# Two attention chunks scored in one burst of TensorE, and three relu copies after it on ScalarE

## The chip, the cores and the metric

The kernel runs on one core of a Trainium2 chip. A core has five engines that run side by side, each with its own queue that it works off in order: TensorE (PE in the profile; its weight loads have a row of their own, PEld), VectorE (DVE), ScalarE (ACT), GpSimd (POOL) and SyncE (SP), which here only issues DMAs. An engine waits for another through semaphores. The metric is the device time of one execution in microseconds; the median over several executions is what two kernels are compared by.

## The reference, cut to what matters

Four batches of 768 tokens pass through two layers. The first is a recurrent attention with a decay for each of 8 heads of 64 numbers; it is computed here in chunks of 128 tokens. The second adds a low-rank mix along the tokens (rank 32) and an MLP from 512 to 2048 and back:

```python
for t in range(S):                                  # S = 768, for each batch and head
    state = gamma * state + outer(k[t], v[t])
    y[t] = scale * q[t] @ state                     # 8 heads of 64 -> x of 512 columns
u = x + (x.T @ U @ V).T                             # U: 768 x 32, V: 32 x 768
out = u + relu(u @ w_ch1) @ w_ch2                   # w_ch1: 512 x 2048, w_ch2: 2048 x 512
```

In chunks, the attention of a chunk is a masked product of its queries and keys (the scores) with its values, plus its queries times the state that the chunks before left behind. The decay is folded into scaled copies of q and v.

## The kernel before, in words

**The order is written out by hand.** The program runs inside a manual schedule, so each engine works in the order in which the Python code emits its instructions. Batch 0's attention runs first, alone, from a list of steps. After it, the MLP of batch b carries the attention of batch b + 1 with it: `mlp_pieces(b)` gives a list of pieces, each with a cost, and `weave` (L404) walks through that list and emits, between two pieces, every function whose mark has been reached. A mark is a share of the MLP's total cost; one whole MLP is 1.0, and the pieces' costs add up to 41.5.

**The pieces of one MLP.** First come 16 up pieces for 512 tokens, each of four matmuls of 512 columns (L356), then 16 up pieces for the other 256 tokens, each of four matmuls of 256 columns, then 24 down pieces of four matmuls of 512 columns (L379). An up piece ends in a relu copy out of its accumulator in PSUM into `gT`: every third one is on VectorE (L361), the others are on ScalarE (L363). Four down pieces make one output chunk, which VectorE adds to `u` (L386) and a DMA that GpSimd issues stores (L342). The accumulators (`mlp`) rotate over three banks of PSUM, so the matmuls of a piece wait for the copy out of the piece that had its bank before, three pieces earlier while nothing else takes a bank.

**One chunk of attention.** `prep_chunk` scales and casts k, q and v on GpSimd (L81, L83) and lets SyncE issue further loads. `turn_chunk` transposes k and q: in batch 1 with TensorE (L230) and a copy by ScalarE (`kT`) and one by VectorE (`qT`), in batches 2 and 3 with a DMA that SyncE issues (L226); `kT` and `qT` have three buffers each. `score` (L234) makes eight matmuls that use 64 of the 128 rows (L239) into one of two accumulators, `R[ci % 2]`, each two banks of PSUM; VectorE then multiplies them by the causal mask into `a` (L242). `mix` (L247) writes into the same `R[ci % 2]`: queries times the state before (L257, 64 rows; none in chunk 0), `a` times the values (L262, 128 rows), and ScalarE copies the result into `x` (L265). Then four matmuls add the chunk's keys times values to the state in PSUM (L274), and two ScalarE copies bring the state out as `ns` (L280), which the next chunk's `mix` reads.

After the six chunks, `lr_proj` (L293), `lr_expand` (L302) and `lr_turn` (in batch 1 on TensorE, L323; later by DMA, L317) make the next batch's `u` and `uT`.

**The marks.** `AT` (L684) holds for each batch the place of the first score, the step from chunk to chunk, the distance from a chunk's score to its mix, and how far ahead `prep_chunk` and `turn_chunk` stand. So in the kernel before, each chunk's scores stand alone between pieces of the MLP, and its mix follows 0.045 or 0.05 of an MLP later.

Of the kernel before, what the change touches and what calls it, by code (L numbers as in the profile page):

```python
# [16 lines left out]
def kernel(  # L17
# [42 lines left out]
    def bank(tag, dtype=fp32):  # L60
        n_bank[0] += 1
        return psum.tile([P, 2048 // (4 if dtype == fp32 else 2)], dtype,
                         tag=tag, name=f"{tag}_{n_bank[0]}", bufs=BANKS[tag])
# [143 lines left out]
    def load_w2(j):  # L207
        nc.gpsimd.dma_start(
            out=w2b[:, ds(4 * j, 4)],
            in_=moe_w_ch2[ds(512 * j, 512)].rearrange("(m p) n -> p m n", p=P))  # L210

    xs = {}
    live = {}
    bts = {}
# [19 lines left out]
    def score(b, ci):  # L234
        r, kT, qT = R[ci % 2], bts.pop(("k", b, ci)), bts["q", b, ci]
        for hp in range(4):
            for i in range(2):
                ri = ds(D * i, D)
                nc.tensor.matmul(r[:, i, ts(hp, P)], kT[ri, hp], qT[ri, hp],  # L239
                                 start=True, stop=True)  # L240
        a = rmid.tile([P, 2, 4, P], bf16, tag="a4", name=f"a4_{b}_{ci}", bufs=3)
        nc.vector.tensor_tensor(  # L242
            a, r.rearrange("p i (n m) -> p i n m", n=4),
            mask[:, None, None, :].to_broadcast([P, 2, 4, P]), op=ALU.mult)
        live["a", b, ci] = a

    def mix(b, ci):  # L247
        if ci == 0:
            open_x(b)
        r, qT = R[ci % 2], bts.pop(("q", b, ci))  # L250
        kb, vb, a = pre.pop(("k", b, ci)), pre.pop(("v", b, ci)), live.pop(("a", b, ci))
        if ci:
            st = live.pop(("state", b, ci - 1))
            for hp in range(4):
                for i in range(2):
                    ri = ds(D * i, D)
                    nc.tensor.matmul(r[:, i, ts(hp, D)], qT[ri, hp],  # L257
                                     st[ri, ts(hp, D)], start=(hp == 0), stop=False,
                                     skip_group_check=True)
        for hp in range(4):  # L260
            for i in range(2):
                nc.tensor.matmul(r[:, i, ts(hp, D)], a[:, i, hp], vb[:, 2 * hp + i],  # L262
                                 start=(ci == 0 and hp == 0), stop=True,
                                 skip_group_check=True)
        evac("A", xs[b][:, ci].rearrange("p (n i e) -> p i n e", i=2, e=D),  # L265
             r[:, :, :256].rearrange("p i (n e) -> p i n e", e=D))
        if ci == NCK - 1:
            return
        if ci == 0:
            live["st_p", b] = bank("st")  # L270
        st_p = live["st_p", b]
        for hp in range(4):
            h2 = ds(2 * hp, 2)
            nc.tensor.matmul(st_p[:, ts(hp, P)], kb[:, h2], vb[:, h2],  # L274
                             start=(ci == 0 and hp == 0), stop=True,
                             skip_group_check=True)
        ns = rmid.tile([P, 4 * D], bf16, tag="ns", name=f"ns_{b}_{ci}")
        for i in range(2):
            ri = ds(D * i, D)
            evac("A", four(ns)[ri], four(st_p)[ri, :, ri])  # L280
        live["state", b, ci] = ns
# [62 lines left out]
    def mlp_pieces(b):  # L344
        gT = gtp.tile([P, NM, S], bf16, tag="gT", name=f"gT_{b}")
        pieces = []
        n = [0]

        def up(m, lo, sz):
            def f():  # L350
                g_p = begun.pop((b, m, lo), None)
                c0 = 2 if g_p is not None else 0
                if not c0:
                    g_p = bank("mlp")
                for c in range(c0, NCB):
                    nc.tensor.matmul(g_p[:, :sz], w1b[:, c, ts(m, P)],  # L356
                                     uTs[b][:, c, ds(lo, sz)], start=(c == 0),
                                     stop=(c == NCB - 1))
                n[0] += 1
                if n[0] % 3 == 0:  # L360
                    nc.vector.tensor_relu(gT[:, m, ds(lo, sz)], g_p[:, :sz])  # L361
                else:
                    nc.scalar.activation(gT[:, m, ds(lo, sz)], g_p[:, :sz],  # L363
                                         AF.Relu)
            return f

        for m in range(NM):
            pieces.append((0.864, up(m, 0, LO)))
        for m in range(NM):
            pieces.append((0.432, up(m, LO, S - LO)))  # L370
        hold = {}

        def down(j, m0, n0=0, nn=DM):
            def f():
                if m0 == 0:
                    hold[j, n0] = bank("mlp")
                ch = hold[j, n0]
                for m in range(m0, m0 + 4):
                    nc.tensor.matmul(ch[:, :nn], gT[:, m, ts(j, P)],  # L379
                                     w2b[:, m, ds(n0, nn)],  # L380
                                     start=(m == 0), stop=(m == NM - 1))
                if m0 == NM - 4:
                    o_sb = outp.tile([P, DM], fp32, tag="o_sb",
                                     name=f"o_{b}_{j}_{n0}")[:, :nn]
                    n = ds(n0, nn)
                    nc.vector.tensor_tensor(o_sb, ch[:, :nn], us[b][:, j, n],  # L386
                                            op=ALU.add)
                    if n0:
                        nc.sync.dma_start(out=out[b, ts(j, P), n], in_=o_sb)
                    else:  # L390
                        stores.append((nc.gpsimd, out[b, ts(j, P), n], o_sb))
            return f

        for j in range(NCK):
            if (b, j) == (B - 1, NCK - 1):
                for n0, nn in ((0, 384), (384, 128)):
                    for m0 in range(0, NM, 4):
                        pieces.append((0.864 * nn / DM, down(j, m0, n0, nn)))
                continue
            for m0 in range(0, NM, 4):  # L400
                pieces.append((0.864, down(j, m0)))
        return pieces
# [18 lines left out]
    def part(f, *args):  # L421
        return lambda: f(*args)
# [258 lines left out]
    for ci in range(3):  # L681
        prep_chunk(1, ci)

    AT = {1: (0.47, 0.068, 0.045, 0.07, 0.04), 2: (0.20, 0.085, 0.05, 0.20, 0.12),  # L684
          3: (0.13, 0.10, 0.05, 0.20, 0.12)}
    LR = {1: (0.875, 0.905, 0.95, 0.975), 2: (0.71, 0.75, 0.83, 0.89)}
    marks = {b: [] for b in range(B)}

    def mark(at, f, *args):
        marks[int(at)].append((at % 1.0, part(f, *args)))  # L690
# [3 lines left out]
        lr_proj(b)  # L694

    for b in range(1, B):
        s0, step, dm, dp, dt = AT[b]
        for ci in range(NCK):
            s_at = b - 1 + s0 + step * ci
            if (b, ci) >= (1, 3):  # L700
                mark(s_at - dp, prep_chunk, b, ci)
            mark(s_at - dt, turn_chunk, b, ci)
            mark(s_at, score, b, ci)
            mark(s_at + dm, mix, b, ci)
            if b > 2:
                mark(b - 2 + 0.25 + 0.1 * ci, open_chunk)
        l0, l1, l2, l3 = LR[min(b, 2)]
        mark(b - 1 + l0, mixed, b)
        mark(b - 1 + l1, lr_expand, b, 0, 4)
        mark(b - 1 + l2, lr_turn, b, 0)  # L710
        mark(b - 1 + l3, lr_turn, b, 2)
        mark(b + 0.02, lr_expand, b, 4, 2)
        mark(b + 0.06, lr_turn, b, 4)
# [35 lines left out]
```

## Time and profile before

| | us |
|---|---|
| median of 3 runs (234.75 to 238.98) | 234.82 |
| the profiled execution | 233.89 |
| its span, first to last instruction | 232.1 |

| engine | busy us | share of the span |
|---|---|---|
| PE | 221.2 | 95% |
| PEld | 120.2 | 52% |
| DVE | 98.4 | 42% |
| ACT | 86.0 | 37% |
| POOL | 77.9 | 34% |

A line of a group has the source line, engine and operation, the tile that is written and those that are read, with shapes; then the number of instructions; then busy us and mean ns of one; then the idle time of the engine just ahead of them and what ended it. The chain is the sequence of work that ended last, in order of time: start, length, what. A timeline line has start, length, engine, what, and in brackets the idle time just ahead and who ended it. Starts and lengths are us from the span's start. The end of a matmul in the timeline contains the time in which it leaves the array, so bursts of different kinds seem to overlap a little; the distance from one start to the next is the time that a burst takes. On ScalarE, too, an instruction can start before the one ahead of it has ended.

The granted TensorE clock is 0.989 over the span, and 1.00 in every stretch of the MLPs that was looked at.

### The profile page before, as it was taken

What the parts mean: (1) busy time and instruction counts of PE and PEld (TensorE: products, weight loads), DVE (VectorE), ACT (ScalarE), POOL (GpSimd) and SP (SyncE); (2) the same over time, 40 slices, a digit from 0 to 9 for tenths busy, and PEclk for the clock granted to TensorE, in tenths of its full rate; (3) what the DMA queues carried; (4) which work ended last, traced back from release to release, by engine and by line L of the source; (5) the groups of instructions that cost most, each with busy time, mean ns of one, the idle gap of its engine ahead of it and who ended that gap; (6) DMA issues with size and microseconds to landing.
All of it is one profiled execution on the core that took longest, in us unless ns stands there. A gap on an engine that the chain in (4) does not pass through costs nothing.

```text
span 232.1 us, 4923 instructions
## 1 busy us (share of the span) xinstructions
PE 221.2 (95%) x2034; PEld 120.2 (52%) x2034; DVE 98.4 (42%) x150; ACT 86.0 (37%) x179; POOL 77.9 (34%) x109
## 2 busy tenths in 40 slices
PE   7789899999999989999999999999999999999992
PEld 2456544685545444467454444477444444674451
DVE  3669646355546433445335244343336143222121
ACT  5474554454443145565320025665210044540000
POOL 4478500373591129850010199530101100000110
PEclk9988999999999999999999999999999999999998
DMA  5999999999999998699899675430112630001212
GB/s 159 298 292 225 204 199 196 220 218 206 228 233 239 248 235 179 101 199 203 144 256 240 136 138 110 95 72 0 37 56 71 160 90 0 3 0 45 90 49 90
DMA packets 92375, 34.61 MB, mean 149 GB/s; under 512 B 77360, under 2 KB 90800, under 8 KB 92352
## 3 DMA queue, kind: packets, MB, share of 16 engines
q1 hardware_dynamic: 86224, 23.86, 51.4%
q0 software_dynamic: 6128, 10.42, 18.4%
q8 instruction: 16, 0.26, 0.5%
q14 instruction: 7, 0.06, 0.1%
HBM read 27.46 MB, written 6.29 MB: 145 GB/s over the span
## 4 chain that ended last, share of the span: by engine, by line
PE 86%; DVE 4%; issue 3%; ACT 3%; POOL 2%; POOLq 0%; DVEq 0%; ACTq 0%
PE mlp L356 36%; PE mlp L379 32%; PE r L262 2%; PE r L239 2%; PE mlp L658 2%; DVE a L510 2%; PE r L257 1%; PE st L274 1%; PE mlp L477 1%; DVE u L309 1%; PE r L503 1%; PE mlp L230 1%; PE r L558 1%; POOL qd L83 1%; PE r L543 1%
## 5 line engine op out<-in xcount | busy, mean ns | idle before, releaser
L379 PE MATMUL mlp<-w2b,gT 128*128 128x512 bf16 (+2 forms) x400 | 88.8, 371 | 0.0
L356 PE MATMUL mlp<-uT,w1b 128*128 128x512 bf16 (+1 forms) x508 | 87.6, 326 | 0.6 <-ACT uT L70 0.2
L363 ACT ACTIVATE gT<-mlp 128x512 bf16<-128x512 f32 (+1 forms) x88 | 42.4, 490 | 68.7 <-PE mlp L356 67.5
L356 PEld LDWEIGHTS <-w1b 128*128 128x128 bf16 x508 | 48.1, 98 | 32.9 <-issue 1.9
L379 PEld LDWEIGHTS <-gT 128*128 128x128 bf16 x400 | 36.6, 98 | 38.3
L342 POOL DMA_DIRECT2D out_dram<-o x24 | 13.3, 553 | 116.0 <-DVE o L386 109.7
L361 DVE TENSOR_SCALAR gT<-mlp 128x512 bf16<-128x512 f32 (+1 forms) x40 | 22.2, 556 | 40.2 <-PE mlp L356 40.2
L242 DVE TENSOR_TENSOR a<-r,mask 128x1024 bf16<-128x1024 f32 x18 | 22.0, 1223 | 26.4 <-PE r L239 23.9
L386 DVE TENSOR_TENSOR o<-mlp,u 128x512 f32<-128x512 f32 (+2 forms) x25 | 16.7, 669 | 38.2 <-PE mlp L379 38.2
L70 ACT ACTIVATE x<-r 128x512 bf16<-128x512 f32 x19 | 11.3, 597 | 25.8 <-PE r L262 25.4
L83 POOL TENSOR_TENSOR qd<-in,gq 128x512 bf16<-128x512 f32 x18 | 18.7, 1040 | 5.0 <-DMA in<-in_q_dram 5.0
L83 POOL TENSOR_TENSOR vd<-in,gk 128x512 bf16<-128x512 f32 x18 | 18.7, 1038 | 0.4 <-DMA in<-in_v_dram 0.3
L81 POOL CAST kd<-in 128x512 bf16<-128x512 f32 x18 | 11.0, 610 | 17.6 <-DMA in<-in_k_dram 11.4
L309 DVE TENSOR_TENSOR u<-r,x 128x512 bf16<-128x512 f32 (+1 forms) x16 | 14.6, 951 | 4.7 <-PE r L302 4.7
L70 ACT ACTIVATE ns<-st 64x256 bf16<-64x256 f32 x30 | 11.1, 372 | 0.3
L510 DVE TENSOR_TENSOR a<-r,mask 128x1024 bf16<-128x1024 f32 x6 | 7.3, 1221 | 2.6 <-PE r L503 2.5
L239 PEld LDWEIGHTS <-kT 64*128 64x128 bf16 x144 | 4.1, 94 | 6.8 <-issue 5.5
L262 PE MATMUL r<-vd,a 128*128 128x64 bf16 x144 | 7.3, 195 | 0.0
L70 ACT ACTIVATE uT<-r 128x1024 bf16<-128x1024 f32 (+1 forms) x5 | 4.7, 937 | 6.8 <-PE r L323 6.1
L239 PE MATMUL r<-qT,kT 64*128 64x128 bf16 x144 | 7.2, 219 | 0.0
L83 POOL TENSOR_TENSOR vu<-in,gk 128x512 bf16<-128x512 f32 (+1 forms) x6 | 6.0, 1003 | 3.0 <-DMA in<-in_v_dram 1.8
L70 ACT ACTIVATE kT<-mlp 128x512 bf16<-128x512 f32 x6 | 3.6, 596 | 7.3 <-PE mlp L230 7.3
(94 smaller groups left out, 132.7 us busy)
## 6 DMA issues: line engine op xcount, KB each, us to landing
in<-in_k_dram SPq DMA_DIRECT2D x24, 256.0 KB, 5.4
in<-in_q_dram SPq DMA_DIRECT2D x24, 256.0 KB, 5.4
in<-in_v_dram SPq DMA_DIRECT2D x24, 256.0 KB, 5.4
out_dram<-o POOLq DMA_DIRECT2D x23, 256.0 KB, 2.9
w1b<-in_moe_w_ch_dram POOLq DMA_DIRECT2D x4, 512.0 KB, 7.7
w2b<-in_moe_w_ch_dram POOLq DMA_DIRECT2D x4, 512.0 KB, 14.6
kT<-kd SPq DMA_TRANSPOSE x12, 3.3
qT<-qd SPq DMA_TRANSPOSE x12, 2.6
```

The costliest lines, as they stand in the source:

```text
L70: nc.scalar.activation(dst, src, AF.Copy)
L83: e.tensor_tensor(dst, src, scale, op=ALU.mult)
L239: nc.tensor.matmul(r[:, i, ts(hp, P)], kT[ri, hp], qT[ri, hp], start=True, stop=True)
L242: nc.vector.tensor_tensor(a, r.rearrange("p i (n m) -> p i n m", n=4), mask[:, None, None, :].to_broadcast([P, 2, 4, P]), op=ALU.mult)
L262: nc.tensor.matmul(r[:, i, ts(hp, D)], a[:, i, hp], vb[:, 2 * hp + i], start=(ci == 0 and hp == 0), stop=True, skip_group_check=True)
L309: nc.vector.tensor_tensor(v4(us[b][:, ds(j0, nj), e]), R[g][:, :, :nj * P].rearrange("p c (j e) -> p c j e", j=nj), v4(xs[b][:, ds(j0, nj) ...
L342: eng.dma_start(out=dst, in_=src)
L356: nc.tensor.matmul(g_p[:, :sz], w1b[:, c, ts(m, P)], uTs[b][:, c, ds(lo, sz)], start=(c == 0), stop=(c == NCB - 1))
L361: nc.vector.tensor_relu(gT[:, m, ds(lo, sz)], g_p[:, :sz])
L363: nc.scalar.activation(gT[:, m, ds(lo, sz)], g_p[:, :sz], AF.Relu)
L379: nc.tensor.matmul(ch[:, :nn], gT[:, m, ts(j, P)], w2b[:, m, ds(n0, nn)], start=(m == 0), stop=(m == NM - 1))
L386: nc.vector.tensor_tensor(o_sb, ch[:, :nn], us[b][:, j, n], op=ALU.add)
```

## The change

For batches 1 to 3, chunks go in pairs (0 and 1, 2 and 3, 4 and 5). Both chunks' `score` now have the same mark, so that no MLP piece stands between them; the two `mix` follow at two distances (`dm` has two values). The places, steps and leads in `AT` change as well. Each call of `score` also fills a list `masks` with three entries; while it has entries, each up piece takes one out, and its relu copy goes to ScalarE even where it is a third piece. Two calls in a row still leave three entries, and entries that are left when the down pieces begin are used up by the first three up pieces of the next MLP. Seven relu copies move from VectorE to ScalarE in this way: the third piece of the MLPs of batches 1, 2 and 3, and one behind each of the first two pairs of batches 2 and 3. In SyncE's queue the order of the DMAs is unchanged. On GpSimd the first two stores of batch 0's outputs each stand one chunk's preparation later in the queue (behind that of chunk 3, and of chunk 4, of batch 1).

```diff
+    masks = []
...
     def score(b, ci):
...
         live["a", b, ci] = a
+        masks[:] = [0, 0, 0]
...
                 n[0] += 1
-                if n[0] % 3 == 0:
+                if n[0] % 3 == 0 and not masks:
                     nc.vector.tensor_relu(gT[:, m, ds(lo, sz)], g_p[:, :sz])
                 else:
                     nc.scalar.activation(gT[:, m, ds(lo, sz)], g_p[:, :sz],
                                          AF.Relu)
+                if masks:
+                    masks.pop()
...
-    AT = {1: (0.47, 0.068, 0.045, 0.07, 0.04), 2: (0.20, 0.085, 0.05, 0.20, 0.12),
-          3: (0.13, 0.10, 0.05, 0.20, 0.12)}
+    AT = {1: (0.46, 0.065, 0.035, (0.04, 0.085), 0.10, 0.06),
+          2: (0.20, 0.085, 0.055, (0.05, 0.095), 0.20, 0.12),
+          3: (0.13, 0.10, 0.07, (0.05, 0.095), 0.20, 0.12)}
...
-        s0, step, dm, dp, dt = AT[b]
+        s0, step, ds_, dm, dp, dt = AT[b]
         for ci in range(NCK):
             s_at = b - 1 + s0 + step * ci
             if (b, ci) >= (1, 3):
                 mark(s_at - dp, prep_chunk, b, ci)
             mark(s_at - dt, turn_chunk, b, ci)
-            mark(s_at, score, b, ci)
-            mark(s_at + dm, mix, b, ci)
+            pair_at = b - 1 + s0 + step * (ci // 2 * 2) + ds_
+            mark(pair_at, score, b, ci)
+            mark(pair_at + dm[ci % 2], mix, b, ci)
```

In the emitted order this makes nine bursts of 16 score matmuls out of eighteen bursts of 8. For batch 2 TensorE's order around the first pair becomes: up pieces, 16 score matmuls, two up pieces (8 matmuls), mix of chunk 0, three up pieces (12), mix of chunk 1, seven up pieces (28, of 256 columns), and the next 16 score matmuls.

## The prediction

> **What bounds the kernel now.** I read the totals and the chain first, then TensorE's part of the chain in order of time, then ScalarE where the chain leaves TensorE, then the groups that the change touches.
>
> The first line of the engines and the shares of the chain:
>
> ```profile
> PE 221.2 (95%) x2034; PEld 120.2 (52%) x2034; DVE 98.4 (42%) x150; ACT 86.0 (37%) x179; POOL 77.9 (34%) x109
> ...
> PE 86%; DVE 4%; issue 3%; ACT 3%; POOL 2%; POOLq 0%; DVEq 0%; ACTq 0%
> ```
>
> TensorE sets the end. So a microsecond counts only if TensorE does less in it, or waits less. What its small bursts cost stands in the chain in order of time (start, length, what):
>
> ```profile
> 64.96 1.06 POOL qd L83
> 66.06 0.40 PE mlp L230 x4
> ...
> 68.97 0.33 PE r L239 x8
> 69.30 0.97 PE mlp L379 x4
> 70.27 0.45 PE mlp L230 x8
> 70.72 0.86 PE mlp L379 x4
> 71.58 0.22 PE r L257 x8
> ...
> 124.63 0.33 PE r L302 x16
> 124.96 10.47 PE mlp L379 x48
> ...
> 186.74 0.22 PE r L302 x8
> ```
>
> Four down matmuls take 0.87 undisturbed (10.47 / 48 x 4), but 0.97 behind a score burst: 0.10 to 0.11 more. The burst itself, eight matmuls of 128 columns on 64 rows, takes 0.33; L257, the same with 64 columns, takes 0.22. So 64 columns more cost 0.11, 128 columns cost 0.22, and 0.11 of each burst is fixed. The L302 rows (32 rows) say the same: 16 matmuls 0.33, 8 of them 0.22, so eight more in the same burst cost only their own 0.11. A score burst costs 0.33 + 0.11 = 0.44, of which half is for going from full-height matmuls to half-height ones and back.
>
> Where the chain leaves TensorE inside an MLP, it goes over ScalarE. Batch 3 behind the mix of chunk 2, in the timeline (engine ACT, then PE):
>
> ```profile
> 154.93 0.60 ACT L70 ACTIVATE x<-r 128x512 bf16<-128x512 f32 x1 [0.64 <-PE r L262]
> 155.43 0.76 ACT L70 ACTIVATE ns<-st 64x256 bf16<-64x256 f32 x2
> 156.21 0.66 ACT L363 ACTIVATE gT<-mlp 128x256 bf16<-128x256 f32 x2
> ```
>
> ```profile
> 156.64 1.03 PE L356 MATMUL mlp<-uT,w1b 128*128 128x256 bf16 x8 [0.21 <-ACT gT L363]
> ```
>
> The copies of a mix hold ScalarE for 1.28 (154.93 to 156.21); the relu behind them frees a bank late, and TensorE waits. From these lines also what ScalarE needs per instruction when it has a queue: x 0.50 to the next start, the two ns 0.78, a relu of 256 columns 0.28 (0.66 for two less 0.38 for one). The groups by shape:
>
> ```profile
> L363 ACT ACTIVATE gT<-mlp 128x512 bf16<-128x512 f32 x44 | 26.2, 597 | 57.0 <-PE mlp L356 56.8
> L242 DVE TENSOR_TENSOR a<-r,mask 128x1024 bf16<-128x1024 f32 x18 | 22.0, 1223 | 26.4 <-PE r L239 23.9 <-ACT gT L363 2.5
> L363 ACT ACTIVATE gT<-mlp 128x256 bf16<-128x256 f32 x44 | 16.5, 382 | 11.7 <-PE mlp L356 10.8
> L361 DVE TENSOR_SCALAR gT<-mlp 128x512 bf16<-128x512 f32 x20 | 13.8, 690 | 25.4 <-PE mlp L356 25.4
> L361 DVE TENSOR_SCALAR gT<-mlp 128x256 bf16<-128x256 f32 x20 | 8.4, 422 | 14.9 <-PE mlp L356 14.9
> ```
>
> **The change part by part.**
>
> *Nine bursts less.* The same 144 score matmuls run in nine bursts. Each merged burst saves the 0.11 inside and the 0.11 behind it: 9 x 0.22 = **-1.98**. If the switch were paid between two chunks too, this is 0; if the columns of the second burst were free as well, 9 x 0.44 = -3.96. I take -1.98, since L302 shows 16 in one burst directly. The bursts of L257, one for each of 15 mixes, stay as many.
>
> *Masks back to back on VectorE.* The first mix of a pair now stands eight matmuls of 512 (1.74) behind the second score burst. Its `a` is ready 0.2 (score to mask) + 1.22 after the first burst, which ends 0.22 before the second: 1.42 against 0.22 + 1.74 = 1.96, so 0.5 is left. The second mask ends at 2.65; the second mix comes at least 2 us after the first. Cost 0. If a VectorE relu of 0.69 is just ahead of the first mask, up to 0.2 a pair is lost, over the four pairs among up pieces 0.8.
>
> *Seven relu copies to ScalarE.* Each takes ScalarE 0.60 or 0.38, VectorE is spared 0.69 or 0.42. Without this, a third piece would stand behind 2.44 of masks. Of itself no cost while ScalarE has time; the next step has the queue. Here the Trainium skill speaks against the change: "ScalarE: Activation LUTs", section "Rules for kernel authors", sends relu to VectorE, up to about three times faster in bf16. The rows above show the reverse for these f32 sources in PSUM, 597 against 690 ns and 382 against 422. By the rule the seven copies would cost ScalarE some 3 x 0.69 each, an estimate, and the time would be some 10 us worse; the rows decide.
>
> *Mixes closer together.* In batch 2 the mixes of chunks 0 and 1 stand three pieces apart (12 matmuls, four of 512 and eight of 256 columns), where 20 matmuls and a score burst stood. ScalarE's queue there, with 0 at the end of chunk 0's L262: the relu of the piece ahead holds it to 0.50, x and ns to 1.78, a relu of 512 to 2.28, one of 256 to 2.56. TensorE meanwhile: L274 0.22, the pieces 1.74 and the switch 0.10, L257 and L262 0.46, so chunk 1's x can start at 2.52 + 0.20 = 2.72 and its ns end at 4.00. The next piece's relu ends at 4.38. TensorE, through with L274 at 2.74 and three pieces of 256 at 4.04, needs that bank: it waits 0.35 to 0.4. At this place of before the 20 matmuls from 103.84 take 2.55 in the timeline, where the 20 from 151.95 take 2.39, so 0.16 to 0.2 was already lost: **+0.2** net. In batch 3 the same sum gives some 0.2 behind the mix of chunk 1 and 0.4 behind that of chunk 2, against two waits of before of about 0.4 (the line at 156.64, with 0.21 more hidden in the burst's own length) and 0.2: 0. In batch 1 one more piece directly follows a pair of TensorE transposes, whose copies take longer than a relu of 256 columns: **+0.15**. Bounds of all this: -0.8 if the waits of before go, since relus then wait for no mask; upwards, every one of the seven moved copies in full, 5 x 0.60 + 2 x 0.38 = 3.8.
>
> *The queues that are passed.* GpSimd prepares chunk 3 of batch 1 before it issues the first store. In before, TensorE waited for q of chunk 4 there (the first two lines of the chain above: qd ends 66.02, the transposes resume at 66.06; 0.30 idle). The two stores now stand behind the preparations instead of ahead: **-0.30**. The second store waits for VectorE's o, which now follows two masks, and chunk 5's preparation (0.57 + 1.0) stands behind it; it ends just about when chunk 5's transposes are reached, so +0.3 instead of -0.30 is the other bound. In batches 2 and 3 SyncE's transposes must land for the second chunk of a pair, whose score is earlier by one step. The tightest is chunk 1 of batch 3: qT is issued at 142.03 and lands 2.6 later by the median (2.4 to 4.7), at 144.6; the score, twelve matmuls of 512 (2.6) behind its old place at 141.73 and one burst, wants it at 144.5. **+0.1**, from 0 to 2.2.
>
> Sum: -1.98 + 0.2 + 0.15 - 0.30 + 0.1 = **-1.8**. Against the profiled execution's own 233.89 (span 232.1 and 1.8 around it) that is 232.1. The runs' median is 234.82, 0.9 above that execution; the difference of kernels should carry over, so 234.8 - 1.8 = **233.0**. A measurement of this kernel can tell about 2%, 4.7 us, from no change: the forecast is a gain that stays within it.
>
> **The rivals.**
>
> *The pair is no single burst* (the change does not do what it says): the second chunk's weights could fall under the same switch because they come from another tile. For it: nothing in before shows two score bursts together. Against: inside a burst each matmul already has its own weights, and L302 x16 goes on at 0.11 per eight across two accumulators. Then only the queues count: +0.15, **235.0**.
>
> *ScalarE becomes the bound* and the kernel is slower. Place: the up pieces of 256 columns in batches 2 and 3, where TensorE takes 0.43 a piece and a mix puts 1.28 of copies into ScalarE's queue. For it: the wait at 156.64. Against: with 0.28 a relu it catches up within some nine pieces. It decides from the point where ScalarE is later than two pieces, 0.87, when the moved copies arrive; then these add in full, and -1.98 + 3.8 - 0.30 + 0.1 = +1.6: **236.4**.
>
> *A transpose by DMA is late* in batch 3's first pair or batch 2's third, whose qT is issued at 111.95 for a score some 3.3 later. For it: by the median landing the one is 0.1 short and the other has 0.7 left. Against: SyncE's order is unchanged, and what it waits for moves with TensorE. At the longest landing, 4.7, the two lose 2.2 and 1.4 and the gain is eaten up: **236.5** at most, 234.5 likely.
>
> **How the numbers follow.** My forecast 0.62 (232.2 to 233.9), no single burst 0.10, a late transpose 0.13, ScalarE 0.15. Two in ten may be left out: the range goes from 231.6, where the waits of before go too (-0.8, the 0.35 is not paid, and each switch may be 0.02 more than read), to 236.5. Faster by over 2% (below 230.1) would need more than every switch of the bursts that go: 0.03. Slower by over 2% (above 239.5) needs ScalarE and the transposes together and something unseen: 0.06. Within 2%: 0.91.
>
> **What would show it.** Right: in the chain L239 x16 at about 0.55, nine times, and down pieces of 0.97 fewer; the 0.30 ahead of L230 gone; a wait of 0.4 for ScalarE some three pieces behind the mix of chunk 1 in batch 2. Wrong: L239 x16 at 0.66; ScalarE's idle time ahead of relus near zero in the stretches of 256 columns; L239 waiting for SyncE; a granted clock that leaves 1.00 in the pairs. What I can't see from here is whether TensorE's clock or DMA timing answers to the new spacing.

## The result, and the profile after

Four executions of the kernel after have a median of 236.86 us (236.34 to 237.41), four of the kernel before 234.94 (234.75 to 238.98). The ratio is 1.012, with an interval of 1.008 to 1.016: a little slower, where 233.0 had been forecast. Here and below, a ratio leaves out executions more than 1.5% above the fastest of their kernel, here that of before at 238.98, which further down turns out to be the one that the four of after should be compared with.

The profiled execution of after takes 237.41, its span is 235.6. First the engines, the clock row, and the chain's shares by engine and by line, from its page:

```profile
PE 218.6 (93%) x2007; PEld 121.9 (52%) x2034; DVE 94.3 (40%) x143; ACT 89.3 (38%) x186; POOL 78.2 (33%) x109
...
PEclk9999659999999999999999999999999999999998
...
PE 81%; SPq 7%; DMA 4%; issue 3%; ACT 2%; DVE 1%; POOLq 0%; POOL 0%
PE mlp L359 35%; PE mlp L384 33%; SPq L108 6%; DMA Uf<-in_moe_U_dram 4%; PE r L265 2%; PE r L241 2%; PE r L260 1%; PE st L277 1%; PE mlp L232 1%; DVE u L312 1%; PE r L305 1%; PE r L326 1%; PE mlp L596 1%; ACT ns L70 1%; PE mlp L337 1%
```

Two things are new: some 10% of the chain lies in SyncE's queue (L108) and in the load of U, which before had no share; and the clock row has two slices at 6 and 5, near 25 to 35 us. Both are in batch 0's attention. No instruction of it is touched: up to the first transpose of batch 1 each engine has the same instructions in the same order in both kernels, and SyncE has them to its end. (Lines of after stand 2 to 5 lower: L239 is L241, L302 is L305, L356 is L359, L379 is L384, L591 is L596.)

The timeline of before around U, SyncE's last load of the start (engine, line, what; in brackets the wait):

```profile
16.35 0.82 SPq L115 DMA_DIRECT2D Uf<-in_moe_U_dram  x1
...
16.87 1.69 POOL L203 DMA_DIRECT2D w1b<-in_moe_w_ch_dram  x2
...
23.51 0.34 ACT L70 ACTIVATE Ub<-Uf 128x192 bf16<-128x192 f32 x1
...
24.05 0.51 PE L591 MATMUL mlp<-x,Ub 128*32 128x128 bf16 x12
```

The same of after, and its stretches with the granted clock (PEclk):

```profile
17.23 0.81 SPq L115 DMA_DIRECT2D Uf<-in_moe_U_dram  x1
...
16.89 1.69 POOL L203 DMA_DIRECT2D w1b<-in_moe_w_ch_dram  x2
...
26.45 0.36 ACT L70 ACTIVATE Ub<-Uf 128x192 bf16<-128x192 f32 x1 [3.52 <-DMA Uf<-in_moe_U_dram]
...
26.87 0.82 PE L596 MATMUL mlp<-x,Ub 128*32 128x128 bf16 x12 [3.47 <-ACT Ub L70]
```

```profile
core 0: us, PE busy (x) PEld busy (x) DVE busy (x) ACT busy (x) POOL busy (x), PEclk, DMA share, GB/s
20.00:24.80 4.80, 2.57 (x70) 1.85 (x70) 4.44 (x6) 1.70 (x3) 4.49 (x6) 1.00 1.36 211
24.80:35.10 10.30, 8.23 (x99) 4.95 (x100) 2.37 (x4) 3.36 (x8) 2.84 (x5) 0.51 1.20 188
```

U's load is issued 0.3 us behind the start of GpSimd's issue of the weights w1, where before it was issued 0.5 ahead of it. It lands at 26.4 instead of 21.1, TensorE stands still for 3.47, and then runs for eight microseconds more at half its clock, which had come down at 25.1, inside the wait. The first burst of 16 matmuls of L305, at the end of batch 0's low-rank part, stands at 42.46 in the chain; in before it stands at 36.76. Of the 5.70, 2.82 come ahead of the matmuls with Ub (26.87 against 24.05) and the other 2.88 behind them.

From that burst of 16 to the last matmul is the part in which the change acts; I call it the **stretch**. It has nothing of batch 0's attention in it. By the starts of the matmuls in the trace, the last row against the row above it:

| stretch, us | to the low-rank part of batch 1 | of batch 2 | of batch 3 | to the last matmul | sum |
|---|---|---|---|---|---|
| before, first profile | 40.92 | 45.52 | 50.23 | 54.18 | 190.85 |
| before, U's load earlier (below) | 40.93 | 45.52 | 50.22 | 53.96 | 190.64 |
| after | 40.11 | 45.04 | 49.52 | 53.96 | 188.63 |
| difference | -0.82 | -0.48 | -0.70 | 0 | -2.01 |

So where the change acts, it gains 2.0 us, and the start of this execution takes 5.7. The chain of after shows the change's signs, the merged bursts and the wait for ScalarE behind the mix of chunk 1 in batch 2 (start, length, what):

```profile
102.02 0.55 PE r L241 x16
...
107.20 0.24 ACT x L70
107.44 0.26 issue
107.69 0.36 ACT ns L70
108.06 0.01 issue
108.07 0.38 ACT ns L70
108.45 0.02 issue
108.47 0.39 ACT gT L366
108.86 0.04 issue
108.91 1.91 PE mlp L359 x16
110.81 0.55 PE r L241 x16
```

A merged burst takes 0.55, nine times. What is left to explain is the start.

### The profile page after: what moved, and what is told of

The parts are those of the page before. It is cut to its first block, busy times and chain, and to the rows that moved or that the text cites. A ratio compares the mean times of both kernels' runs of the same rounds, so it can differ in the third digit from the quotient of the medians.

```text
span 235.6 us, 4893 instructions
## 1 busy us (share of the span) xinstructions
PE 218.6 (93%) x2007; PEld 121.9 (52%) x2034; DVE 94.3 (40%) x143; ACT 89.3 (38%) x186; POOL 78.2 (33%) x109
## 4 chain that ended last, share of the span: by engine, by line
PE 81%; SPq 7%; DMA 4%; issue 3%; ACT 2%; DVE 1%; POOLq 0%; POOL 0%
PE mlp L359 35%; PE mlp L384 33%; SPq L108 6%; DMA Uf<-in_moe_U_dram 4%; PE r L265 2%; PE r L241 2%; PE r L260 1%; PE st L277 1%; PE mlp L232 1%; DVE u L312 1%; PE r L305 1%; PE r L326 1%; PE mlp L596 1%; ACT ns L70 1%; PE mlp L337 1%
## 5 line engine op out<-in xcount | busy, mean ns | idle before, releaser
L359 PE MATMUL mlp<-uT,w1b 128*128 128x256 bf16 (+1 forms) x501 | 86.4, 325 | 1.2 <-ACT gT L366 0.4
L384 PE MATMUL mlp<-w2b,gT 128*128 128x512 bf16 (+2 forms) x384 | 85.7, 370 | 1.3 <-issue 0.6
L366 ACT ACTIVATE gT<-mlp 128x512 bf16<-128x512 f32 (+1 forms) x95 | 45.9, 493 | 64.6 <-PE mlp L359 63.5
L359 PEld LDWEIGHTS <-w1b 128*128 128x128 bf16 x508 | 48.6, 98 | 33.4 <-issue 1.8
L384 PEld LDWEIGHTS <-gT 128*128 128x128 bf16 x400 | 37.0, 98 | 39.3 <-issue 0.2
L364 DVE TENSOR_SCALAR gT<-mlp 128x256 bf16<-128x256 f32 (+1 forms) x33 | 18.0, 545 | 45.0 <-PE mlp L359 45.0
L244 DVE TENSOR_TENSOR a<-r,mask 128x1024 bf16<-128x1024 f32 x18 | 21.2, 1220 | 6.4 <-PE r L241 5.2
L83 POOL TENSOR_TENSOR qd<-in,gq 128x512 bf16<-128x512 f32 x18 | 18.8, 1042 | 5.9 <-DMA in<-in_q_dram 5.9
L515 DVE TENSOR_TENSOR a<-r,mask 128x1024 bf16<-128x1024 f32 x6 | 7.3, 1222 | 2.2 <-PE r L508 2.1
L72 DVE CAST qT<-mlp 128x512 bf16<-128x512 f32 x6 | 4.1, 690 | 6.0 <-PE mlp L232 5.8
L265 PEld LDWEIGHTS <-a 128*128 128x128 bf16 x144 | 5.4, 98 | 1.2
L277 PE MATMUL st<-vd,kd 128*128 128x128 bf16 x60 | 5.8, 219 | 0.0
```

The costliest lines, as they stand in the source:

```text
L83: e.tensor_tensor(dst, src, scale, op=ALU.mult)
L244: nc.vector.tensor_tensor(a, r.rearrange("p i (n m) -> p i n m", n=4), mask[:, None, None, :].to_broadcast([P, 2, 4, P]), op=ALU.mult)
L359: nc.tensor.matmul(g_p[:, :sz], w1b[:, c, ts(m, P)], uTs[b][:, c, ds(lo, sz)], start=(c == 0), stop=(c == NCB - 1))
L366: nc.scalar.activation(gT[:, m, ds(lo, sz)], g_p[:, :sz], AF.Relu)
L384: nc.tensor.matmul(ch[:, :nn], gT[:, m, ts(j, P)], w2b[:, m, ds(n0, nn)], start=(m == 0), stop=(m == NM - 1))
```

## The experiments

My theory: the change does what was forecast, and the first comparison measured which of two starts an execution had. The rival: something in the change (the spacing, the program's place in memory, the clock's answer to it) slows the kernel.

**The kernel after again, unaltered.** No edit.

> The changed kernel once more, unaltered, beside the kernel before. Theory A (the pairs gain about 2 us, and a race at the start, in which the load of U lands behind the first load of w1, costs 4 to 5.5 us): again about 236.3 to 237.4 where U lands at about 26, about 232.8 where it lands at about 21. Theory B (the new order itself costs time in batches 1 to 3): 236.3 to 237.4 whenever U lands. Theory C (the first chip was at fault): about 233, with U at 21.

Six executions: 231.58 (231.13 to 231.89), ratio 0.991 (0.987 to 0.994). U is issued at 16.53, ahead of w1, and nothing waits for it; the stretch is 188.67, the same as in the first profile. The same program can be 5 us faster than at first, and in the profiles it is so by its start alone.

**U's load earlier, in both kernels.** SyncE issues it behind v of chunk 3 instead of last:

```diff
-    for step in ("k0 q0 v0 k1 q1 v1 k2 q2 v2 k3 q3 v3 k4 q4 k5 q5 v4 v5 ").split():
-        load_unit(step[0], int(step[1]))
-    nc.sync.dma_start(out=Uf, in_=moe_U.rearrange("(j p) r -> p j r", p=P))
+    for step in ("k0 q0 v0 k1 q1 v1 k2 q2 v2 k3 q3 v3 U k4 q4 k5 q5 v4 v5 ").split():
+        if step == "U":
+            nc.sync.dma_start(out=Uf, in_=moe_U.rearrange("(j p) r -> p j r", p=P))
+        else:
+            load_unit(step[0], int(step[1]))
```

> The kernel before, with the load of U issued six loads earlier (behind v3 in place of last), so that no load of w1 can come ahead of it. Theory A: 234.5 to 235.2, as the kernel before, since U landed early there already; the clock at 0.989. Theory B: the same. If it is over 236, the earlier load delays k4 to v5 and the tool is no good.

> The changed kernel with the same earlier load of U. Theory A: 232.3 to 233.3, that is 1.5 to 2.5 under the one before with the same edit, granted clock back at 0.989. Theory B: 236 to 237, still 1 to 2 over the kernel before. Theory C: as the changed kernel on this chip.

Before with this start: 233.83 (232.54 to 234.88, 10 executions), stretch 190.64. After with it: 232.96 (231.76 to 235.40, 10), stretch 188.63. The stretches differ by 2.01, the medians by 0.9, where 1.5 to 2.5 had been expected. The unaltered kernel before had 7 of 22 executions at 238 to 240 on this occasion; with U early neither kernel had one above 235.4.

**U late in the kernel before.** Its load is issued behind the first w1 load, by way of a GpSimd write that it has to wait for:

```diff
-    nc.sync.dma_start(out=Uf, in_=moe_U.rearrange("(j p) r -> p j r", p=P))
...
+        if mb == 0:
+            nc.gpsimd.memset(Uf[:1, 0, :1], 0.0)
+            nc.sync.dma_start(out=Uf, in_=moe_U.rearrange("(j p) r -> p j r", p=P))
```

> The kernel before, with U's load held back until the first load of w1 has been issued (a write of one number of U's tile by GpSimd, behind that load's issue, is what it waits for). Theory A: the start is lost here as well, in every run: 238.5 to 240.5, granted clock about 0.975, a wait of 3 us or more for U ahead of the copy Ub, and a stretch of half clock behind it. Theory B: U's landing costs at most the 3 us of the wait, 234.8 to 237.8, or nothing.

Four executions take 235.54, 240.05, 240.40 and 240.58 (median 240.22), so the late issue doesn't cost the start every time, as had been expected. The one at 240.05 was profiled and gives the same picture as after's first profile, in a kernel without the change: U lands some 5 us later than in its first profile, the first burst of 16 stands at 43.15 instead of 36.76, the stretch is 190.64. Its timeline and its stretches:

```profile
26.28 0.36 ACT L70 ACTIVATE Ub<-Uf 128x192 bf16<-128x192 f32 x1 [1.01 <-DMA Uf<-in_moe_U_dram]
...
26.69 0.64 PE L593 MATMUL mlp<-x,Ub 128*32 128x128 bf16 x12 [0.95 <-ACT Ub L70]
```

```profile
20.00:26.70 6.70, 4.84 (x133) 3.40 (x132) 6.30 (x8) 3.50 (x8) 6.53 (x8) 1.00 1.30 206
26.70:36.90 10.20, 10.20 (x104) 5.36 (x104) 2.68 (x5) 3.47 (x8) 0.18 (x1) 0.51 1.21 193
```

TensorE waits for under 1 us here, where 3 or more had been expected, and the clock is halved for ten all the same.

**The parts of the change, one at a time.** Pairs without the moved copies (`masks` stays empty), the moved copies without pairs, and pairs whose second score stands a little later, so that a piece can come between:

```diff
-        masks[:] = [0, 0, 0]
```

```diff
 before, and:
+        masks[:] = [0, 0, 0]
...
-                if n[0] % 3 == 0:
+                if n[0] % 3 == 0 and not masks:
...
+                if masks:
+                    masks.pop()
```

```diff
-            mark(pair_at, score, b, ci)
+            mark(pair_at + 0.015 * (ci % 2), score, b, ci)
```

> The changed kernel without the moved relu copies: every third copy stays on VectorE. Read by the stretch from the first low-rank burst of 16 (batch 0) to the last matmul, which the start does not touch: 190.85 before, 188.63 changed. If the moved copies do what the prediction says (a copy behind 2.44 us of masks holds a bank): TensorE waits 1.2 to 1.7 behind the second pairs of batches 2 and 3, stretch 190.5 to 192. Rival, the moved copies are idle: 188.5 to 188.8.

> The kernel before with the moved relu copies alone: scores one chunk at a time, old places. If the gain is that of the merged bursts: stretch 190.4 to 191.3. Rival, the gain comes from the moved copies: 188.6 to 189.8.

> The changed kernel with one or two MLP pieces between the two score bursts of a pair, all else as it is. If a switch between full and half height costs 0.22 for each burst: nine more bursts, 9 x 0.22 = 2.0, stretch 190.2 to 191.0. Rival, the gain comes from the new places of the mixes and the GpSimd order: 188.6 to 189.2.

One execution each, all three with a late start (237.98, 238.55, 238.21), so only the stretch counts. *Without the copies* it is 189.01: the copies on ScalarE are worth 0.38, where I had expected that the pairs need them for about 2 us or more. The masks hold VectorE long enough only for two more waits of 0.2 in the stretches of 256 columns (the 20 matmuls behind batch 2's second pair take 2.55 instead of 2.36). *The copies alone*, eleven here and not seven, since each score by itself fills the list, give 190.19, a gain of 0.45 on 190.64 without any pair. Two waits of 0.2 of before are gone here, one in batch 2 and one in batch 3, each behind a mask that held up a relu on VectorE (the 20 matmuls from 103.84 of before take 2.55, here 2.36). *The split pairs* give 189.91, 1.28 of the gain back. The expectation had nine pairs split; in the chain three are still one burst, since 0.015 doesn't always reach over the next piece's end. Batch 2's second pair there:

```profile
110.61 0.33 PE r L241 x8
111.92 0.33 PE r L241 x8
```

Six split pairs cost 1.28, so 0.213 for each burst; 0.22 was forecast.

**Other distances, and w1 later.** The mixes of chunks 1 and 3 of batches 2 and 3 stand 0.02 later; GpSimd's first two w1 loads are issued behind the casts of q and v of chunk 5 (`w0` and `w1` in the list of steps):

```diff
-        "... Tk4 m3 Q4 ST3.1 w0 s3.1 Tq4 K5 kT4 w1 M3 "
-        "qT4 Tk5 FS4:1 x3 Q5 S4 kT5 V4 Tq5 qT5 xt0 m4 V5 ST4.0 Ub S5 s4.0 P0 m5 "
+        "... Tk4 m3 Q4 ST3.1 s3.1 Tq4 K5 kT4 M3 "
+        "qT4 Tk5 FS4:1 x3 Q5 w0 S4 kT5 V4 Tq5 qT5 xt0 m4 V5 w1 ST4.0 Ub S5 s4.0 P0 m5 "
...
-            mark(pair_at + dm[ci % 2], mix, b, ci)
+            mark(pair_at + dm[ci % 2] + (0.02 if b > 1 and ci in (1, 3) else 0), mix, b, ci)
```

> Two edits on the changed kernel. In batches 2 and 3 the mixes of chunks 1 and 3 come 0.02 of an MLP later, so that ScalarE has two pieces more between two mixes: the waits of 0.40, 0.19 and 0.40 for a relu copy should go, stretch 187.6 to 188.1 where the changed kernel has 188.63; if the waits only move, 188.5 to 188.8. And the first two loads of w1 are issued one GpSimd cast and three casts later, behind U's load: if the race at the start is what makes the slow runs, no run above 234.5, median 230.5 to 232.5; if it is something else, some runs at 235 and more again.

235.63 (235.23 to 237.47), ratio 1.009 (1.003 to 1.014). Both ideas miss. The start is good (first burst of 16 at 36.5 and no wait for U), but the kernel lets batch 1's inputs go only when the third w1 load has landed; they are issued at 31.94 instead of 29.83, batch 1's transposes wait for them, and batch 1's part takes 43.76 instead of 40.11. The waits behind the mixes only move: batch 2's part takes 45.07, batch 3's 49.73.

**The kernel after a third time, and U two places earlier in both.**

```diff
-    for step in ("... k4 q4 k5 q5 v4 v5 ").split():
+    for step in ("... k4 q4 k5 q5 U v4 v5 ").split():
```

> The changed kernel unaltered on a third occasion. If the place where U lands is drawn anew in each execution and does not depend on the change: a mixture of about 231 to 232 (U at 21 to 22, clock 0.99 and more) and 236 to 237.5 (U at 25 to 26, clock 0.97 to 0.98), the slow ones about as frequent as in the kernel before, which shows 1 in 3 to 1 in 5. If the change makes the late start: nearly all at 236 to 237.5 while the kernel before is mostly at 233 to 235.

> The changed kernel with U's load two places earlier, ahead of v4 and v5, w1 as it is. If the order of U and w1 makes the two starts: no execution above 235, median 231 to 232.5, U landed by 22 and ahead of w1. If the slow start has another cause: some executions at 236 to 237.5 again.

> The kernel before with the same edit: 233 to 234.5 and no execution at 238 to 240. Against it the changed kernel with the edit is 1.8 to 2.4 faster, which is what the change is worth when the start is the same; the stretch from the first low-rank burst of 16 to the last matmul 190.6 to 190.9 here and 188.6 to 188.7 there.

The unaltered kernel after: 232.94 (232.32 to 237.00, 12 executions), against 233.32 for before; ratio 0.999 (0.996 to 1.002), stretch 188.63. One of its executions is at 237.0, the others at 232.3 to 234.6. U two places earlier doesn't help: 235.47 for after (ratio 1.004, 0.999 to 1.008) and 236.21 for before (1.008, 1.004 to 1.012), 0.7 apart where 1.8 to 2.4 had been expected. In the profiles the stretch of before is 190.65, as expected, and that of after 191.62 instead of 188.6: batch 1's transposes wait for their inputs, and two merged bursts of batch 2 are torn by waits for qT of 0.29 and 0.54. Now v of chunk 5 is last in SyncE's queue, and it is this load that falls behind w1. The chain of before with it:

```profile
17.65 9.93 DMA in<-in_v_dram
...
27.73 1.06 POOL vu L83
```

It is issued 0.9 behind the start of w1's issue and takes 9.9 us. With U's load early it is last in the queue as well, but issued at 15.2 in the second such profile of after (below), ahead of w1, and takes 6.6. So it isn't U: whichever load comes last is late if w1 gets ahead of it.

The start of its issue doesn't decide that. In the run of the pairs without copies and in that of the copies alone, U's issue starts 1.0 ahead of w1's, but it takes 2.2 and 2.0 instead of 0.8, and U lands at 26.1 and 25.5 all the same. The first of them:

```profile
15.40 2.22 SPq L115 DMA_DIRECT2D Uf<-in_moe_U_dram  x1
...
16.45 1.70 POOL L203 DMA_DIRECT2D w1b<-in_moe_w_ch_dram  x2
```

The end of its issue sorts all 18 profiles: in the seven in which the last load lands at 24.5 or later, its issue ends 0.9 to 1.7 behind the start of w1's; in the other eleven, in which it lands by 22.4, at most 0.5 behind it. In five of the late ones this issue or the one ahead of it takes 2.0 to 2.8, in the others 1.7 at most; why, the runs don't show.

**Both kernels with w1 behind all of SyncE's loads.** `w0` and `w1` as above, and the gate reads the second w1 load instead of the third, so that batch 1's inputs are let go no later:

```diff
-    nc.gpsimd.tensor_copy(out=gate[:1, :1], in_=w1b[:1, NCB - 1, 1535:1536])
+    nc.gpsimd.tensor_copy(out=gate[:1, :1], in_=w1b[:1, NCB - 1, 1023:1024])
```

> The kernel after, with GpSimd's first two w1 loads issued later (the first behind the cast of q of chunk 5, the second behind the cast of v of chunk 5), so that U's load stands ahead of both; the inputs of batch 1 wait for the second w1 load instead of the third, so that they come as early as before. If the start alone made the first result, no execution has a late U and none is above 235; the stretch from the first burst of 16 matmuls of batch 0 to the last matmul takes 188.6, and the median is 230.5 to 232.5, some 2 us below the same start in the kernel before. If the change itself makes slow starts, some executions are at 236 or more here too. If batch 1's inputs still come late, the stretch is 190 or more.

> The kernel before, with the same edit of the start. If the start alone made the slow executions at 238 to 240, none is left; the stretch takes 190.6 and the median is 232.5 to 234.5, 1.8 to 2.4 above the kernel after with this start. If slow executions have another cause, they are here as often as in the kernel before, about one in five.

Both profiles have an early start, and none of the 12 executions of before is above 236.47, while 3 of 23 of the unaltered kernel are at 238.9 to 239.6. For after the times don't show it: three of 12 are at 236.73 to 236.92, where its late starts lie, and were not profiled. After takes 235.40 (234.02 to 236.92; ratio 1.006, 1.002 to 1.010) and before 235.14 (1.004, 1.001 to 1.007): with this start the change gains nothing, where some 2 had been expected, and the stretch of after is 193.16, that of before 191.25. After's timeline shows where (batch 1's first two transposes, then the first and the third merged burst of batch 2, each torn in two):

```profile
48.43 0.40 PE L232 MATMUL mlp<-ident,qd 128*128 128x128 bf16 x4 [1.98 <-POOL qd L83]
...
52.62 0.40 PE L232 MATMUL mlp<-ident,qd 128*128 128x128 bf16 x4 [0.88 <-POOL qd L83]
...
98.18 0.40 PE L241 MATMUL r<-qT,kT 64*128 64x128 bf16 x8
99.23 0.40 PE L241 MATMUL r<-qT,kT 64*128 64x128 bf16 x8 [0.66 <-DMA qT<-qd]
...
117.41 0.40 PE L241 MATMUL r<-qT,kT 64*128 64x128 bf16 x8
118.48 0.40 PE L241 MATMUL r<-qT,kT 64*128 64x128 bf16 x8 [0.67 <-DMA qT<-qd]
```

GpSimd waits 6.05 for the q of chunk 0 there (until 47.33), so the first transpose waits too. The change puts that transpose earlier (0.40 of an MLP instead of 0.43; in its other profiles 10.3 us behind the first burst of 16, in before 11.6) and the second score of a pair one step earlier. With inputs on time this costs nothing; with late inputs it is 1.3 us less of slack, and waits appear which the kernel before has only in part.

**U early once more, and batch 1 moved back.** The pair with U behind v of chunk 3 again, with more executions, and after with

```diff
-    AT = {1: (0.46, 0.065, 0.035, (0.04, 0.085), 0.10, 0.06),
+    AT = {1: (0.475, 0.065, 0.035, (0.04, 0.085), 0.10, 0.06),
```

> The kernel before with U's load behind that of v of chunk 3, once more. Stretch 190.6, the median 233.3 to 234.3, no execution above 236.

> The kernel after with the same start. If the gain in the stretch arrives whole, the median is 1.8 to 2.2 below the kernel before with this start. If it arrives only in executions whose inputs are on time, the median is 0.5 to 1.2 below, the fastest executions are some 2 below the fastest of the other, and the slowest are no faster. No execution above 236.

> The same, with the first score of batch 1 at 0.475 of the MLP instead of 0.46: its first two pairs of transposes stand 0.6 us later, one piece or two. If waiting for batch 1's inputs takes a part of the gain, the median is 0.3 to 0.6 below the unshifted one, and its slowest executions come down. If what is missing lies in batch 0's start or in batch 2's transposes by DMA, it stays within 0.2.

Before: 234.83 (232.35 to 235.07, 12 executions), after: 233.08 (231.74 to 236.65, 12); their stretches are 190.63 and 188.62. The medians are 1.75 apart, the fastest executions 0.6, and one of after is at 236.65, where its late starts lie. With the two runs above, 22 executions of each: means of 234.19 and 233.29, 0.9 apart (0.2 to 1.5). So about half of the 2.0 arrives. The shifted kernel takes 233.70 (232.90 to 235.06), 0.6 more and not less: a miss. Its profile has an early start (first burst of 16 at 36.4, in the unshifted one at 38.0) and a stretch of 190.94. The third w1 load lands later there, the gate opens at 31.60 instead of 29.87, and batch 1's transposes wait; what the start gains, the inputs take back, and a shift that moves the first transpose by 0.4 (10.75 behind the first burst of 16 instead of 10.31) is too small for a delay of 1.7.

**All executions of the two kernels together.** The times of before have a gap in which nothing lies. Before: 100 executions at 232.12 to 235.56, median 233.87, and 17 at 237.97 to 239.93, median 239.04. After: 17 at 231.13 to 234.57, median 232.90, and 5 at 236.34 to 237.41, median 236.93, four of them those of the first comparison. Like with like, the change gains 1.0 with the early start and 2.1 with the late one. That fits the rest: after a late start the inputs have five microseconds more to arrive. But both the gain and the share of late starts change with the occasion: with the early start the medians are 1.9 apart when after was run again and 0.4 when it was run a third time, and of before 1 of 4, 7 of 22, 2 of 10, 4 of 29, 3 of 23 and 0 of 29 executions are late.

## Why the prediction was wrong

**The step that failed** is the last one of the sum: "the difference of kernels should carry over, so 234.8 - 1.8 = 233.0". It took batch 0 for the same in both, and had no term for a start that can come out in two ways, 5 us apart, although the times of before already showed it (two at 234.8 and one at 238.98). In its place the runs showed a gain of 2.0 where the change acts and, in the first profile, 5.7 lost ahead of it; of the four executions of after in the comparison the profiled one has the late start, and the times of the other three fit it. The sentence on TensorE's clock and DMA timing asked whether they answer to the new spacing; the clock did change, but ahead of the pairs, in a part that the change doesn't touch. The upper end of the range, 236.5, would have had to hold a late start.

**Against the other steps, by part** (forecast terms, then measured): batch 1, -0.66 + 0.15 - 0.30 = -0.81, measured -0.82; batch 2, -0.66 + 0.2 = -0.46, measured -0.48; batch 3, -0.66 + 0 + 0.1 = -0.56, measured -0.70. In detail:

- *Nine bursts less.* 0.553 for 16 matmuls, forecast 0.55; 0.213 saved for each by the split pairs, forecast 0.22. Right, and the rival "no single burst" falls.
- *Seven relu copies to ScalarE at no cost of their own.* Right, and by themselves they gain 0.38 (by taking them away) to 0.45 (in the run with eleven of them alone). These are the two waits of 0.2 behind masks; the forecast had their end in the net of the mixes, so the gain doesn't come on top of the terms above. The groups of after show ScalarE still the faster:

```profile
L366 ACT ACTIVATE gT<-mlp 128x512 bf16<-128x512 f32 x49 | 29.0, 597 | 54.2 <-PE mlp L359 54.2
L364 DVE TENSOR_SCALAR gT<-mlp 128x512 bf16<-128x512 f32 x15 | 10.4, 690 | 28.5 <-PE mlp L359 28.5
```

  So the Trainium skill's rule that was weighed ("ScalarE: Activation LUTs", section "Rules for kernel authors") doesn't hold for these copies, and the rival "ScalarE becomes the bound" falls as well.
- *Mixes closer together.* The wait behind the mix of chunk 1 is there: 28 matmuls of 256 columns take 3.53 from 107.22 to 110.75, of which 28 x 0.107 = 2.99 are their own and 0.10 the switch; 0.44 is left, 0.35 to 0.4 was forecast.
- *The stores passed on GpSimd.* POOL leaves the chain (2% before, 0% after), and batch 1's transposes take 0.28 less in sum (3.18 against 3.46, in two profiles with an early start): -0.30 was right.
- *A late transpose.* Not in the first profile, whose batch 3 has only bursts of 0.55. But this is the rival that the later runs bring back: with w1 late, and with U two places earlier, two of batch 2's bursts wait for qT. The forecast had looked at batch 2's third pair and batch 3's first; the first of batch 2 it had not.

So the 2.0 of the stretch was right, 1.8 forecast, and the time was not. With an early start the kernel after takes 232.90; that this is next to the forecast's 233.0 is luck, since before takes 233.87 with it, and 1.0 of the 1.8 arrives.

**What stays open.** Why the first comparison drew the late start four times in four, where 17 of 117 executions of before and 1 of the 18 others of after have it. The queues are the same up to the first transpose of batch 1; what differs is the program behind it. That the change makes late starts more frequent isn't shown, and not excluded; nor was it tested whether the chip of the first comparison has a part in it. Which executions with an early start lose part of the 2.0 to their inputs is argued from the profiles of altered kernels; those that were lost in the unaltered one were not profiled.

## What to carry to other kernels

Compare two kernels stage by stage, from a mark that both share, before explaining a difference: here "1% slower" hid a gain of 2.0 in one stage and, in the profile, a loss of 5.7 in another that nobody touched. When the times of a kernel have a gap, a forecast needs each of its groups and their shares, not a median. And a change that starts a stage earlier spends the slack of that stage's loads; look up what their landing has left before counting the gain.

## What the runs showed of the hardware

**The last load of a queue, issued next to another queue's large load.** U's 96 KB land 4.8 us after the start of their issue in before (16.4 to 21.1) and 9.2 in after (17.2 to 26.4); v of chunk 5, 256 KB, takes 6.6 ahead of w1 and 9.9 behind it. In before U's packets begin to move at 18.55, ahead of w1's first at 19.13; in after w1's begin at 19.00 and U's at 20.25. From then on both queues move nearly as many packets, but U's are of 128 bytes and w1's of about 1 KB, so U gets a small part of the bytes. From 21.6 to 25.0 of after, GpSimd's queue and then SyncE's (packets, MB, share):

```profile
q0 software_dynamic: 635, 0.62, 112.0%
q1 hardware_dynamic: 614, 0.08, 26.3%
```

**The clock can stay at half while TensorE is busy.** In the run without moved copies ScalarE waits 0.35 for U, TensorE hardly at all, and the clock is at half from 15.6 to 36.1 (a stretch, with the granted clock ahead of the last two columns):

```profile
15.40:35.90 20.50, 19.82 (x267) 12.37 (x266) 11.21 (x14) 8.00 (x17) 10.06 (x14) 0.51 1.23 211
```

In before the same dip begins at about 15.4 and ends at about 18.8:

```profile
15.10:18.60 3.50, 3.46 (x52) 2.10 (x44) 1.99 (x3) 1.47 (x3) 3.46 (x5) 0.54 1.21 291
```

The Trainium skill, "TensorE: Matmul & The Clock Gate", section "Why this matters for your kernels", asks for no idle gap of TensorE above some 3 us between bursts and says that a window of idle brings half the clock. The 3.47 in after is such a gap, though the clock was at half from 25.1, when TensorE had stood still for 1.7. The 0.95 in before with U late is none, and 20.5 us at half the clock with TensorE busy for 19.82 of them don't fit either; here the measurement decides. What these stretches have in common is batch 0's short dependent bursts; which of their properties counts wasn't tried.
